# An H3-plus-MLP kernel on one core: the hand-written order of its second part is written anew

## The chip, the cores and the metric

The kernel runs on one core of a Trainium2 chip. The time is device microseconds for one execution; before the change three runs gave a median of 238.91 us (238.69 to 239.14). Five engines work side by side: TensorE (PE, with its weight loads shown apart as PEld), VectorE (DVE), ScalarE (ACT), GpSimd (POOL), and SyncE (SP), which here only issues DMA transfers.

## The reference: what is computed

Four residual blocks follow each other on x of shape 1 x 2048 x 512. Two kinds alternate, A, B, A, B, with the same weights each time.

```
A: k_shift = 4-tap causal FIR of k along the sequence, a filter per channel
   kv      = k_shift * v
   y       = causal convolution of kv with ssm_k (2048 taps per channel, by FFT) + kv * ssm_D
   x       = x + layernorm(x) * y
B: h = gelu_tanh(layernorm(layernorm(x)) @ w1 + b1)      # 512 -> 1376
   x = x + h @ w2 + b2                                    # 1376 -> 512
```

k, v and ssm_k do not depend on x, so y is the same in both A blocks and is computed once. Everything is bfloat16 with f32 accumulation.

## The kernel before, in words

The sequence is cut in two halves of 1024 positions. For each half the long convolution is done as a transform by matmuls: a first stage (`stage1`, matmuls at L557), a second stage (`stage2`, matmuls at L569), a product in the frequency domain on DVE (`tt`, L468), and two inverse stages (`inverse1`, L674, and `inverse2`, L696), which give y. The FIR is a set of matmuls with diagonal weights (`shift_pair`, L642, in the second half), and its product with v is DVE's L651. For the second half the products of the transforms ("p2" and "x2_1" in the code) are added by DVE ("sum", L468 too), and `inverse1` reads the sums. Each first- or second-stage result leaves PSUM through `evac`, which is ACT's L473 or DVE's L474.

The MLP works on row tiles of 128 positions, put together into row blocks: in the first half two blocks of one tile and seven of two tiles, in the second half four blocks of four tiles. For each block: statistics (`stats`: DVE L810 and L811, then POOL L815 and L817 for 1/sqrt, then L820, whose form on DVE the profile shows as L822 and whose form on POOL as L825), the normalisation (`norm`: ACT L835 or DVE L836), the product with y and the residual sum (DVE L468), statistics and normalisation again, a transpose (a DMA transpose issued by SP at L879, for the first two tiles PE's L887), then 11 groups of four matmuls of the first MLP matmul (L899), each followed by ACT's gelu (L904), and 11 matmuls per row tile of the second (L933, in three groups of 4, 4 and 3), followed by DVE's residual sum (L937). The last row tile is cut into pieces of 256, 128 and 128 columns (L922, L926).

Nothing is scheduled at run time. Every operation is recorded once in a `Prog`, and three tables decide the rest. `SEQ` lists all 1185 operations in one global order; each engine executes its own in that order. `ENGS` has a letter for each operation that two engines can do. `BANKS` gives each PSUM tile its place in the eight banks; a tile that gets a bank waits until the previous owner was read. `sync` then derives every semaphore wait from the data and from the banks. So a table changes when things happen and on which engine, and never what is computed.

```
self.seq = [self.ops[i] for i in self.SEQ]
o.eng = ... {"a": ACT, "v": DVE, "p": POOL}[next(choice)]      # letters of ENGS
t.base = int(b)                                                # digits of BANKS
```

Of the kernel before, what the change touches and what calls it, by code (L numbers as in the profile page):

```python
# [36 lines left out]
class Prog:  # L37
# [62 lines left out]
    ENGS = (  # L100
            "avapapvpaavvaavaavaaaaavvvvapvppvavvavaavaavvaaaaaaaavaaaaaaaaavaavaaaaaapvpvaaaaaaaaaaaaaaaaaaaaaaaaaaa"
            "aappappaavpvppaappvvppaapvaappaappaappaappaappavppvappaapvaappvvppvappvapvvvaapvavavvvvavvvvvvvvpvvvvvvv"
            "aavvpvaavvvvavvv")
    BANKS = (
            "45704306202464200000627236026646246464226006402420624644066042640262264660244620204426464644246204266020"
            "22247020226337626301520172570440464475725755436672367720371021321620440063513741720454430362521124671007"
            "27743140661373223714364027332203342000120556367705202105351567170234501404453107474")

    def __init__(self, nc):
        self.nc = nc  # L110
# [863 lines left out]
```

## Time and profile before

| | |
|---|---|
| median of 3 runs | 238.91 us (238.69 to 239.14) |
| the profiled execution's own time | 238.14 us |
| its span in the trace | 236.3 us |
| busy: PE, PEld, DVE, ACT, POOL | 222.5, 146.9, 179.2, 159.2, 49.1 us |
| matmuls recorded | 2743 |
| granted TensorE clock | 1.00 of full speed over the whole span |

The span is what the trace shows between the first and the last instruction; 1.84 us of the profiled execution's time lie outside it. Start times below are microseconds from the span's start. The chain of waits (called "the chain" below) follows the last instruction back, at each step to what released it. A few matmul records are missing from the trace, and each missing one looks like a gap of some 50 ns in PE's busy time though PE went on.

### The profile page before, as it was taken

The numbers are of one execution on the slowest core, as the hardware profiler recorded it, in microseconds if no ns is written. First come the engines' busy times: TensorE is split into PE (matmuls) and PEld (weight loads), VectorE is DVE, ScalarE is ACT, GpSimd is POOL, SyncE is SP. The second block draws the span as 40 slices with busy tenths as digits, with TensorE's granted clock in tenths as the row PEclk, the third lists the DMA queues.
The fourth block names the chain that finished last, engine by engine and source line by source line (L and its number), as shares of the span: only waits on it lengthen the run. The fifth ranks groups of instructions, "written<-read, shape, count | busy, mean of one in ns | idle before, by whom it ended". The sixth has DMA issues, their size and how long they took to land.

```text
span 236.3 us, 6496 instructions
## 1 busy us (share of the span) xinstructions
PE 222.5 (94%) x2743; PEld 146.9 (62%) x2765; DVE 179.2 (76%) x364; ACT 159.2 (67%) x254; POOL 49.1 (21%) x104
## 2 busy tenths in 40 slices
PE   6898787998999999999999999999999999999995
PEld 3787677876958578567867567644444444444444
DVE  0679979999999999999999899593179779521122
ACT  2963899998969679999787999556047204913520
POOL 1450020914222215321204432101020120100000
PEclk9999999999999999999999999999999999999999
DMA  6999879893869620032500212401200030173102
GB/s 213 299 390 385 304 213 287 250 284 69 171 124 254 142 47 3 0 49 52 172 0 6 44 26 53 105 0 29 60 1 3 13 76 0 22 114 133 44 0 92
DMA packets 41113, 26.77 MB, mean 113 GB/s; under 512 B 23702, under 2 KB 33788, under 8 KB 41084
## 3 DMA queue, kind: packets, MB, share of 16 engines
q1 hardware_dynamic: 40786, 26.20, 40.0%
q8 instruction: 22, 0.36, 0.6%
q10 hardware_dynamic: 298, 0.16, 0.3%
q14 instruction: 7, 0.06, 0.1%
HBM read 15.07 MB, written 2.10 MB: 73 GB/s over the span
## 4 chain that ended last, share of the span: by engine, by line
PE 65%; DVE 17%; ACT 7%; SPq 4%; DMA 3%; issue 2%; DVEq 0%
PE ps L933 27%; PE ps L899 27%; DVE ar L468 12%; ACT ar L473 6%; DMA ar<-in_A_v_dram 3%; SPq L453 3%; PE ps L569 2%; PE ps L557 2%; PE ps L696 2%; PE ps L674 2%; DVE ar L474 1%; ACT ar L904 1%; DVE ar L620 1%; PE ps L922 1%; DVE sm L810 1%
## 5 line engine op out<-in xcount | busy, mean ns | idle before, releaser
L904 ACT ACTIVATE ar<-ps,sm 128x256 bf16<-128x256 f32 (+5 forms) x143 | 65.8, 523 | 37.5 <-PE ps L899 37.3
L899 PE MATMUL ps<-ar 128*128 128x256 bf16 (+5 forms) x568 | 81.8, 297 | 0.5 <-ACT ar L473 0.2
L473 ACT ACTIVATE ar<-ps 128x1024 bf16<-128x1024 f32 (+3 forms) x77 | 71.8, 1003 | 14.0 <-PE ps L557 4.7
L933 PE MATMUL ps<-ar 128*128 128x512 bf16 (+1 forms) x325 | 76.2, 379 | 1.4 <-issue 0.6
L899 PEld LDWEIGHTS ps<-ar 128*128 128x128 bf16 (+1 forms) x572 | 52.7, 100 | 27.8 <-ACT ar L904 0.7
L468 DVE TENSOR_TENSOR ar<-ar 128x512 bf16<-128x512 bf16 (+3 forms) x105 | 62.9, 636 | 3.0 <-ACT ar L835 1.7
L933 PEld LDWEIGHTS ps<-ar 128*128 128x128 bf16 (+1 forms) x341 | 32.5, 98 | 35.9 <-ACT ar L904 0.4
L810 DVE BATCH_NORM_STATS2 sm<-ar 128x6 f32<-128x512 bf16 x64 | 42.4, 682 | 0.4
L937 DVE TENSOR_TENSOR ar<-ar,ps 128x512 bf16<-128x512 bf16 x31 | 20.6, 678 | 29.2 <-PE ps L933 29.0
L835 ACT ACTIVATE ar<-ar,sm 128x512 bf16<-128x512 bf16 x33 | 25.9, 808 | 13.2 <-DVE sm L822 10.6
L817 POOL TENSOR_TENSOR sm<-sm 128x2 f32<-128x2 f32 (+2 forms) x26 | 21.4, 822 | 32.5 <-DVE sm L815 30.7
L815 POOL TENSOR_SCALAR sm<-sm 128x2 f32<-128x2 f32 (+2 forms) x21 | 6.1, 293 | 91.2 <-DVE sm L811 90.9
L557 PE MATMUL ps<-ar 128*64 128x128 bf16 x512 | 17.5, 221 | 2.4 <-POOL ar L468 1.1
L569 PE MATMUL ps<-ar 128*128 128x64 bf16 x512 | 17.9, 193 | 1.7 <-ACT ar L473 1.3
L569 PEld LDWEIGHTS ps<-ar 128*128 128x128 bf16 x512 | 16.6, 98 | 3.8 <-ACT ar L473 1.8
L474 DVE CAST ar<-ps 128x1024 bf16<-128x1024 f32 x13 | 15.8, 1219 | 2.9 <-PE ps L569 1.8
L557 PEld LDWEIGHTS ps<-ar 128*64 128x64 bf16 x512 | 14.8, 110 | 5.0 <-POOL ar L468 1.2
L674 PE MATMUL ps<-ar 64*128 64x64 bf16 (+1 forms) x384 | 12.6, 203 | 0.5 <-ACT ar L473 0.3
L674 PEld LDWEIGHTS ps<-ar 64*128 64x128 bf16 (+1 forms) x384 | 11.9, 114 | 1.9 <-ACT ar L473 1.2
L836 DVE TENSOR_SCALAR ar<-ar,sm 128x512 bf16<-128x512 bf16 x31 | 12.0, 407 | 0.8 <-POOL sm L825 0.5
L767 DVE SCALAR_TENSOR_TENSOR ar<-ar,sm,ps 128x512 bf16<-128x512 bf16 x16 | 10.7, 743 | 0.4 <-PE ps L569 0.4
L811 DVE BATCH_NORM_AGGREGATE sm<-sm 128x2 f32<-128x6 f32 x64 | 10.1, 171 | 0.6
(42 smaller groups left out, 90.0 us busy)
## 6 DMA issues: line engine op xcount, KB each, us to landing
ar<-tab_s SPq DMA_DIRECT2D x16, 256.0 KB, 7.9
ar<-ar SPq DMA_DIRECT2D x16, 256.0 KB, 4.3
ar<-in_A_ssm_k_dram SPq DMA_DIRECT2D x8, 256.0 KB, 6.7
ar<-in_A_q_dram SPq DMA_DIRECT2D x8, 256.0 KB, 4.6
ar<-in_A_v_dram SPq DMA_DIRECT2D x8, 256.0 KB, 6.3
out_dram<-ar SPq DMA_DIRECT2D x7, 256.0 KB, 2.4
ar<-in_B_w_dram SPq DMA_DIRECT2D x4, 344.0 KB, 5.2
ar<-in_B_w_dram SPq DMA_DIRECT2D x5, 256.0 KB, 4.4
```

The costliest lines, as they stand in the source:

```text
L468: return P.op(eng, lambda e: e.tensor_tensor(o, a, b, op), dur, reads=[a, b] + list(more), writes=[o])
L473: return e.activation(dst, src(), AF.Copy)
L557: r = e.matmul(Q(tl, 64 * ri, 64, i * 128, [1, 128]), w, m, start=True, stop=True)
L569: r = e.matmul(Q(tl, 0, 128, i // 8 * 512 + i % 8 * 4, [32, 16], [1, 4]), w, m, start=True, stop=True)
L674: r = e.matmul(Q(tl, 0, 128, i, *([32, 16], [1, 4]) if split else ([1, 128],)), w, m, start=n == 0, stop=n == 1)
L810: P.op(DVE, lambda e, sj=sj, x=x: e.bn_stats(sj, x), 600.0, reads=[x], writes=[sj])
L817: P.op(POOL, lambda e: e.tensor_tensor(r, v, hf, ALU.pow), 420.0 + 149.0 * n, reads=[v, hf], writes=[r])
L835: return e.activation(o, x, AF.Identity, bias=u, scale=r)
L899: r = e.matmul(Q(tl, 0, rows, 0, [1, w]), a, m, start=dk == 0, stop=dk == 3)
L904: P.op(ACT, lambda e, dst=dst, tl=tl, rows=rows, bias=bias, w=w: e.activation(dst, Q(tl, 0, rows, 0, [1, w]), AF.Gelu_apprx_tanh, bias=bia ...
L933: r = e.matmul(Q(tl, 0, 128, 0, [1, 512]), ins[fc][0], ins[fc][1], start=fc == 0, stop=fc == 10)
L937: P.op(DVE, lambda e, x=x, tl=tl: e.tensor_tensor(x, x, Q(tl, 0, 128, 0, [1, 512]), ALU.add), 604.0, reads=[x], writes=[x], tile=tl)
```

## The change

Only the three tables differ. The first 330 entries of `SEQ` are the same, which is everything up to about 60.7 us of the trace; the other 855 are in a new order, on every engine. 23 operations behind that point go to another engine: of the ACT-or-DVE normalisations nine go from DVE to ACT and four from ACT to DVE; of the small statistics steps that DVE or POOL can do, seven go from DVE to POOL and three the other way. The banks of most tiles behind the same point are new. No operation is added or removed, and the shapes are the same. A line or two of each table:

```diff
     SEQ = (
         ...
-        424, 413, 404, 421, 259, 450, 405, 422, 288, 451, 408, 480, 423, 452, 415, 456, 483, 460, 457, 481, 446, 453,
...
+        424, 387, 413, 422, 425, 259, 408, 421, 452, 288, 466, 409, 480, 418, 453, 416, 467, 483, 448, 417, 481, 456,
...
     ENGS = (
...
-            "aappappaavpvppaappvvppaapvaappaappaappaappaappavppvappaapvaappvvppvappvapvvvaapvavavvvvavvvvvvvvpvvvvvvv"
-            "aavvpvaavvvvavvv")
+            "aappappaavpvppaappvvppaapvaappaappaapvaappaappavppvappaappaappvvppaappvappaaavvvvvaappvaaapvvvavpvvvavpp"
+            "aavvvvvaavvvvvvv")
     BANKS = (
-            "45704306202464200000627236026646246464226006402420624644066042640262264660244620204426464644246204266020"
...
+            "45704306202464200000627236026646246464226006402420624644066042640262264600644466440666002624266260062444"
...
```

**PE, where the first transform stage of the second half (L557, `stage1` with tag "x1_1") stands among the MLP's matmuls (L899 and L933).** Before, from the second group of L557 to the last:

```order
L557 MATMUL ps<-ar 64x128 x16
L899 MATMUL ps<-ar 128x256 x36
L899 MATMUL ps<-ar 96x256 x4
L899 MATMUL ps<-ar 128x256 x4
L899 MATMUL ps<-ar 96x256 x4
L899 MATMUL ps<-ar 128x256 x4
L557 MATMUL ps<-ar 64x128 x32
L933 MATMUL ps<-ar 128x512 x4
L899 MATMUL ps<-ar 128x256 x4
L557 MATMUL ps<-ar 64x128 x32
L933 MATMUL ps<-ar 128x512 x8
L557 MATMUL ps<-ar 64x128 x32
```

And now, from the second group of L557 to the last:

```order
L557 MATMUL ps<-ar 64x128 x48
L933 MATMUL ps<-ar 128x512 x8
L557 MATMUL ps<-ar 64x128 x48
L933 MATMUL ps<-ar 128x512 x7
L557 MATMUL ps<-ar 64x128 x16
```

In both orders one more group of 16 stands ahead of these, right behind L642. So the eight steps of 16 matmuls are in five groups before and in four now, and the L899 matmuls that stood between them stand ahead of them.

**DVE, the frequency-domain products and sums of the second half (L468 with 128x32x64) that the inverse transform (L674) waits for.** Before:

```order
L468 TENSOR_TENSOR ar<-ar 128x32x64 x2
L811 BN_AGGR sm<-sm 128x2
L468 TENSOR_TENSOR ar<-ar 128x32x64 x3
L822 SCALAR_TENSOR_TENSOR sm<-sm 128x2
L468 TENSOR_TENSOR ar<-ar 128x32x64
L937 TENSOR_TENSOR ar<-ar,ps 128x512
L468 TENSOR_TENSOR ar<-ar 128x32x64 x6
```

And now:

```order
L811 BN_AGGR sm<-sm 128x2
L468 TENSOR_TENSOR ar<-ar 128x32x64 x3
L937 TENSOR_TENSOR ar<-ar,ps 128x512
L468 TENSOR_TENSOR ar<-ar 128x32x64 x2
L937 TENSOR_TENSOR ar<-ar,ps 128x512
L468 TENSOR_TENSOR ar<-ar 128x32x64 x10
```

The small statistics steps (L811, L822) have left the middle of the run, and the last ten products and sums stand in one piece where six stood.

**POOL, the statistics of the row block whose L811 is the one just shown (the eighth block, "q7" in the code).** Before:

```order
L825 TENSOR_SCALAR sm<-sm 128x1 x2
L815 TENSOR_SCALAR sm<-sm 128x2
L817 TENSOR_TENSOR sm<-sm 128x2
L851 MEMSET ar 1x512
L815 TENSOR_SCALAR sm<-sm 128x2
L817 TENSOR_TENSOR sm<-sm 128x2
```

And now:

```order
L815 TENSOR_SCALAR sm<-sm 128x2
L817 TENSOR_TENSOR sm<-sm 128x2
L825 TENSOR_SCALAR sm<-sm 128x1 x2
L815 TENSOR_SCALAR sm<-sm 128x2
L851 MEMSET ar 1x512
L817 TENSOR_TENSOR sm<-sm 128x2
```

The step that was L822 on DVE is now the L825 pair on POOL: the block has four POOL instructions in a row where it had two.

More of the change, by code (lines that the diff above doesn't have):

```diff
@@ L58 @@
         244, 257, 584, 403, 585, 443, 249, 410, 412, 586, 406, 207, 411, 250, 444, 213, 407, 420, 293, 445, 258, 414,
[41 rows of a table removed]
[41 rows of a table added]
     ENGS = (
             "avapapvpaavvaavaavaaaaavvvvapvppvavvavaavaavvaaaaaaaavaaaaaaaaavaavaaaaaapvpvaaaaaaaaaaaaaaaaaaaaaaaaaaa"
-            "aappappaavpvppaappvvppaapvaappaappaappaappaappavppvappaapvaappvvppvappvapvvvaapvavavvvvavvvvvvvvpvvvvvvv"
-            "aavvpvaavvvvavvv")
+            "aappappaavpvppaappvvppaapvaappaappaapvaappaappavppvappaappaappvvppaappvappaaavvvvvaappvaaapvvvavpvvvavpp"
+            "aavvvvvaavvvvvvv")
     BANKS = (
-            "45704306202464200000627236026646246464226006402420624644066042640262264660244620204426464644246204266020"
-            "22247020226337626301520172570440464475725755436672367720371021321620440063513741720454430362521124671007"
-            "27743140661373223714364027332203342000120556367705202105351567170234501404453107474")
+            "45704306202464200000627236026646246464226006402420624644066042640262264600644466440666002624266260062444"
+            "46206466216237643301320727321504123101100322332716373063445423545175402012133355426403067156573421254373"
+            "47061653171314250227620662421047670120016563423216502311505064403200454166210125364")
     def __init__(self, nc):
```

80 rows, old and new, of the table SEQ are left out of this document.

## The prediction, made before the changed kernel was run

> **What bounds the kernel now.** I read the page first, then the busy time by stretches, then the chain of waits, and last the weight loads' waits. The page says who works all the time:
>
> ```profile
> span 236.3 us, 6496 instructions
> PE 222.5 (94%) x2743; PEld 146.9 (62%) x2765; DVE 179.2 (76%) x364; ACT 159.2 (67%) x254; POOL 49.1 (21%) x104
> PEclk9999999999999999999999999999999999999999
> ```
>
> PE is busy for 94% at full clock. The change begins at about 60.7 us, so I cut the time behind it into stretches that end where the kernel's character changes (123.26 us is the end of DVE's run of products and sums, 160 us the point from which only MLP work is left). The columns are the stretch, its length, and each engine's busy time:
>
> ```profile
> 60.00:80.00 20.00, 19.79 (x334) 14.72 (x339) 19.59 (x44) 16.28 (x41) 4.18 (x12) 1.00 0.83 190
> 80.00:100.00 20.00, 19.52 (x305) 14.68 (x297) 19.91 (x35) 17.89 (x32) 6.64 (x14) 1.00 0.13 22
> 100.00:123.26 23.26, 23.10 (x264) 17.07 (x265) 22.99 (x30) 21.11 (x39) 4.25 (x7) 1.00 0.30 69
> 123.26:160.00 36.74, 36.15 (x442) 23.04 (x446) 32.65 (x90) 28.55 (x48) 8.93 (x18) 1.00 0.17 38
> 160.00:230.00 70.00, 69.68 (x320) 31.98 (x325) 34.53 (x89) 28.16 (x45) 5.94 (x8) 1.00 0.18 42
> 230.00:236.30 6.30, 3.77 (x39) 2.79 (x38) 2.01 (x5) 0.00 (x0) 0.00 (x0) 1.00 0.27 86
> ```
>
> PE's idle time is 0.21, 0.48, 0.16, 0.59 and 0.32 us in the first five stretches. In the fifth no other engine is busy for half of the time and the chain is PE throughout, so I take its 0.32 us for missing records: they are not to be had. That leaves 1.44 us. An order can neither remove a matmul nor shorten one, so **1.44 us and what the switches between kinds of matmul cost is all that this change can gain**, some 0.6% of the time. What it can lose has no such bound: DVE is busy 62.49 of the 63.26 us from 60 to 123.26 us, and PE has little to do without it at the seam between the halves.
>
> **The change part by part.** *Switches.* A piece of the chain of waits (start, length, work), where L557 stands alone between L899:
>
> ```profile
> 83.81 2.62 PE ps L899 x24
> 86.43 0.57 PE ps L557 x16
> 87.00 5.78 PE ps L899 x52
> 92.79 1.01 PE ps L557 x32
> ```
>
> Twenty-four L899 take 2.62 us, 0.109 each; 52 of them should take 5.68 and take 5.78, so coming back costs 0.10. A lone group of 16 L557 takes 0.57 us, two together 1.01: the second one costs 0.44, so going in costs 0.13. A round trip is 0.2 us, and five groups become four: **-0.2 us**. The number of groups of L642 and of L674 does not change. At worst the rest of the cost stays hidden behind other waits: 0 to -0.2.
>
> *The front, 60.7 to 70 us.* Here PE does the first half's small groups of L899 faster than ACT does the gelus that empty their banks. The waits of the weight loads in this stretch, and the chain:
>
> ```profile
> PEld ps L899 <- ACT ar L904: 0.5, 2, 0.3
> ...
> 60.53 1.74 ACT ar L904 x6
> ...
> 62.27 0.63 ACT ar L904 x2
> 62.91 0.05 issue
> 62.95 0.84 PE ps L899 x12
> ```
>
> The chain lies on ACT's gelus until 62.91 us, so PE is paced by them. A weight load waits in 0.5 us of which PE, which has earlier matmuls in its pipe, loses a part. The new order has the first L569 after 36 more L899 instead of 48, and eight L899 instead of four before the next one, so ACT gets its pause earlier. Nothing in it removes a gelu. Bounds: all 0.5 comes back, or the waits move and grow by half of that (+0.25). I take **-0.15 us**, nearer to the lower half of the gain since ACT remains full.
>
> *The seam, L674.* Each of the eight steps fills two PSUM banks and waits for ACT to empty earlier ones. PE's timeline there, and the waits of its weight loads from 100 to 160 us:
>
> ```profile
> 124.47 2.56 PE L674 MATMUL ps<-ar 64*128 64x64 bf16 x128
> 127.19 1.46 PE L933 MATMUL ps<-ar 128*128 128x512 bf16 x6 [0.16 <-DVE sm L811]
> 128.58 2.56 PE L674 MATMUL ps<-ar 64*128 64x64 bf16 x128
> 131.30 1.89 PE L933 MATMUL ps<-ar 128*128 128x512 bf16 x8 [0.16 <-issue]
> ...
> PEld ps L674 <- ACT ar L473: 0.8, 3, 0.4
> ```
>
> Both groups take 2.56 us, with up to 0.8 us of waits for ACT in them, and the gaps of 0.16 us behind them. The new order keeps two groups of four steps with seven L933 between them, and all eight evacuations on ACT. The same loop of PE, ACT and bank stands there again: I take **-0.05 us**, between -0.4 (half of the waits go) and +0.4 (half as many again).
>
> *Ahead of the seam, DVE against PE.* Between the divergence and the first L674 the two orders hold the same PE work, and the same DVE work but for one L822 that leaves and one that comes. What is in cover there:
>
> ```profile
> 116.37 7.23 DVE L468 TENSOR_TENSOR ar<-ar 128x2048 bf16<-128x2048 bf16 x7
> 123.52 0.69 DVE L810 BATCH_NORM_STATS2 sm<-ar 128x6 f32<-128x512 bf16 x1
> ```
>
> DVE's last sum ends before 123.52 and L674 starts at 124.47: 0.95 us of cover. PE comes up to 0.4 us earlier by the terms above, which leaves about 0.5. So this costs **nothing** as long as DVE is not more than 0.5 us later than now; if it is, L674 waits for it, and behind L674 the inverse, the next statistics and the next row block's transposes.
>
> *Normalisations and statistics moved between engines* shift DVE's load in the second half to ACT and POOL. There PE has 69.68 of 70 us of work queued and DVE and ACT half of theirs: **nothing**, covered by the m2 matmuls (L933); without that cover a four-tile step on POOL instead of DVE would be 1 us on the path of its block. On SP's queue the transposes keep their order but for neighbours, and three stores of finished rows move behind the last transposes:
>
> ```profile
> out_dram<-ar SPq DMA_DIRECT2D x7, 256.0 KB, 2.4
> ```
>
> Nothing waits for them but the end, some 20 us later: nothing. *The end*, behind 230 us, has the same pieces (three of L922, the sums, the last stores): 0.
>
> The sum: -0.2 - 0.15 - 0.05 = **-0.4 us**. From the profiled execution's own 238.14 us (236.3 of span, 1.84 around it) this makes 237.7; the median of the runs lies 0.77 above that execution, so **238.5 us** is what I expect of the median, 0.17% under 238.91. About 0.2%, 0.48 us, is what a measurement of this kernel can tell from no change, so my forecast lies inside it, near its edge.
>
> **The rivals.** *The gain is given back.* The new order puts L569 steps singly between L899 from 101 to 116 us, each with an evacuation on ACT, which is busy 21.11 of 23.26 us there: a gelu that stands behind an evacuation frees its bank later by that much. Ten places at 0.03 to 0.06 us are +0.3 to +0.6, and the time is 238.7 to 239.2, around 238.9. For it speaks ACT's load, against it that PE's idle time in that stretch is only 0.16 us today, with the same evacuations on ACT.
>
> *DVE is late at the seam (slower).* The products wait for evacuations (their row in DVE's timeline, the first pair of the second half's products):
>
> ```profile
> 102.90 2.36 DVE L468 TENSOR_TENSOR ar<-ar 128x2048 bf16<-128x2048 bf16 x2 [0.23 <-ACT ar L473]
> ```
>
> In the new order the second-stage steps come to PE one by one, and the product of each can start only when its evacuation is through. If DVE waits in this run as for this pair but at six places instead of one, that is 6 x 0.23 = 1.4 us later, 0.9 beyond the cover; L674 waits, and with it the block behind it. It decides from 0.5 us of delay; at 1.4 the time is 238.5 + 0.9 = 239.4, with the front's gain gone too 239.6. Against it: the new order leaves DVE nothing else between the products, so that none is queued behind a statistic.
>
> *GpSimd is shut out (slower).* The profile shows what a run of two-input products on DVE can do to a small POOL instruction:
>
> ```profile
> 40.24 6.11 DVE ar L468 x10
> ...
> 41.32 5.41 POOL L632 COPY ar<-ar 128x3 bf16<-128x3 bf16 x2 [7.74 <-PE ps L557]
> ...
> 98.44 0.33 POOL L815 TENSOR_SCALAR sm<-sm 128x2 f32<-128x2 f32 x1 [3.68 <-DVE sm L811]
> ...
> 111.23 1.07 POOL L815 TENSOR_SCALAR sm<-sm 128x2 f32<-128x2 f32 x1 [8.82 <-DVE sm L811]
> 112.39 1.57 POOL L817 TENSOR_TENSOR sm<-sm 128x2 f32<-128x2 f32 x1
> ```
>
> Two copies of three elements take 5.41 us and are through only when the ten L468 are; the same L815 takes 0.33 us alone and 1.07 beside the products. The new order has the four POOL instructions of one block start at this run, and ten L468 in one piece at its end (10 x 1.2 = 12 us). If the last of the four is shut out until the run ends at about 123.3 us, the two normalisations on ACT that need it hold up ACT from about 119, and with it the gelus whose banks PE wants: some 4 us, 242.5. It decides if the four are not through when the ten begin, near 112 us. Between the block's L811 and the ten stand five products and two L937, some 7 us, so the four would each have to lose more than the 1.07 and 1.57 us of the rows at 111 us. The Trainium skill ("SBUF — State Buffer", section "Who interferes with whom") says that a VectorE tensor_tensor with both inputs in SBUF contends with a GpSimd instruction that reads SBUF, and that whoever issues first holds the shared ports for the whole instruction. By that rule each of the four waits for one product, 1.2 us, and all are done before the ten begin: no cost. The rows at 111 us agree with it, and the row at 41.32, which outlasts eight products, is worse than it.
>
> *All of it comes back.* If the new order removed every wait, 1.44 us: 237.5. Against it the loop at L674, which stands as it was.
>
> **How the numbers follow.** My forecast (238.2 to 238.7) gets 0.40, the gain given back 0.24, a larger gain (237.5 to 238.2) 0.12, DVE late at the seam 0.18, GpSimd shut out 0.06. Faster by over 0.2% means below 238.43: the larger gain and 0.26 of the forecast, 0.38. Within 0.2%: the other 0.14 and the gain given back, 0.38. Slower: 0.24. The range is 237.7 to 239.6: it leaves out the hold, the far end of the larger gain and half of the late DVE, about 0.17 in all. The likeliest case's own range is 238.2 to 238.7.
>
> **What would show it.** The switches: four groups of L557 in PE's timeline, and a lone group still at 0.57. The front: the weight loads' wait for L904 between 60 and 70 us under 0.5 us. The seam: L674 still 2.56 us a group, its first start about 0.3 us earlier than 124.47, and DVE's last sum before it. GpSimd: the L815 to L825 of that block through before 112 us. In the stretch from 160 to 230 us PE 69.7 us busy as now. The prediction is wrong if PE's idle time behind 60 us has grown by more than half a microsecond, or fallen by more than one.

## The result, and the profile after

| | before | after |
|---|---|---|
| median on the same chip | 238.91 us (238.06 to 240.06, 9 runs) | 237.40 us (236.53 to 238.17, 9 runs) |
| ratio | 1 | 0.9929 (0.9904 to 0.9955) |
| the profiled execution's own time | 238.14 us | 237.62 us |
| its span | 236.3 us | 235.8 us |

The kernel became faster by 0.71%, some 1.5 us. The prediction had 238.5 us and a range from 237.7: the direction of its sum was right, the gain is larger, and the time lies 0.3 us below the range. In 33 of 325 executions of these kernels the granted clock is 0.993 instead of 1.0 and the time is longer, by 1.4 us on the mean, so a median of some ten runs moves by a few tenths with their number.

The page of the kernel after, who works all the time:

```profile
span 235.8 us, 6520 instructions
PE 223.4 (95%) x2765; PEld 146.6 (62%) x2765; DVE 177.0 (75%) x355; ACT 161.7 (69%) x259; POOL 55.2 (23%) x117
```

All 2765 matmuls are recorded in this trace; before, 22 records were missing. Records go missing with the trace and not with the kernel: two of the four repeats of the kernel after (below) lack 22 as well. The busy time by stretches (stretch, length, then the busy time of PE, PEld, DVE, ACT and POOL):

```profile
60.00:80.00 20.00, 20.00 (x330) 14.90 (x331) 19.97 (x44) 16.42 (x42) 4.36 (x13) 1.00 0.85 178
80.00:100.00 20.00, 20.00 (x313) 14.89 (x301) 19.68 (x36) 17.90 (x33) 7.57 (x11) 1.00 0.24 38
100.00:123.26 23.26, 23.26 (x278) 17.18 (x278) 22.61 (x28) 21.63 (x38) 5.66 (x11) 1.00 0.27 70
123.26:160.00 36.74, 36.63 (x447) 23.01 (x446) 30.62 (x83) 31.14 (x52) 12.06 (x27) 1.00 0.15 30
160.00:229.50 69.50, 69.50 (x327) 32.09 (x326) 34.00 (x84) 27.76 (x46) 6.61 (x12) 1.00 0.19 46
```

PE's idle time in these stretches fell from 1.76 to 0.11 us. That is not 1.65 us of gain, nor any part of it. A repeat of the kernel after (a_rep1) that lacks 22 records is idle for 1.75 us in the same five stretches (busy for 167.75 of 169.50 us), although its steps start at the same times, to 0.01 us, as in the trace that shows 0.11. So nearly all of the 1.76 us before is missing records too, some 0.08 us for each, and not the 50 ns given ahead. What the order gained is read from the starts of PE's steps. At some places both orders have done exactly the same set of PE steps, and there the two can be compared. Microseconds from the same L899 at 60 us, worked out from the starts of PE's matmuls (at 131 us of a weight load, where the matmul's record is missing) in three traces of the kernel before and two of the kernel after:

```
                            before   repeat   repeat    after   repeat   difference
77.8 us, behind the FIR     17.914   17.911   17.912   17.684   17.683     -0.23
83.4 us                     23.575   23.571   23.572   23.298   23.297     -0.28
121.1 us, ahead of L674     61.277   61.280   61.271   60.651   60.650     -0.63
127.6 us                    67.765   67.768   67.756   67.143   67.142     -0.62
131.1 us, behind the seam   71.216   71.218   71.214   70.603   70.598     -0.62
191.5 us                   131.606  131.608  131.605  130.990  130.989     -0.62
the last matmul's end      173.967  173.969  173.963  173.351  173.350     -0.62
```

The stretch behind 60 us is the same from execution to execution to 0.01 us, and the change is worth 0.62 us in it. At 103.9 us, behind the last L557 group, the two profiled executions are 0.50 us apart (43.990 against 43.486, at the first step behind the same work). So 0.28 us come up to 83 us, 0.23 from there to 104 us, 0.12 from there to 121 us, and nothing at the L674 groups or behind them: the first L674 starts 0.62 us earlier already (64.612 against 63.989). From the last matmul to the span's end it is 2.52, 2.74 and 2.52 us before, and 2.40 and 2.41 us after (2.39 to 2.41 in five traces).

The front first. The weight loads of the kernel after wait for nothing at all between 60 and 70 us; the 0.5 us of waits for L904 are gone. ACT's timeline there, before and then after, shows how:

```profile
60.53 4.15 ACT L904 ACTIVATE ar<-ps,sm 128x128 bf16<-128x128 f32 x15
64.53 0.84 ACT L835 ACTIVATE ar<-ar,sm 128x512 bf16<-128x512 bf16 x1
```

```profile
60.73 3.59 ACT L904 ACTIVATE ar<-ps,sm 128x128 bf16<-128x128 f32 x13
64.17 0.85 ACT L835 ACTIVATE ar<-ar,sm 128x512 bf16<-128x512 bf16 x1
```

ACT's run of gelus is two shorter, and PE, which has eight L899 between its L569 instead of four, no longer waits for a bank. Between 104 and 121 us a wait of the same kind got shorter, that of an L569 for a gelu. The weight loads' waits from 100 to 160 us, before and then after:

```profile
PEld ps L569 <- ACT ar L904: 0.4, 1, 0.4
```

```profile
PEld ps L569 <- ACT ar L904: 0.2, 1, 0.2
```

Before, that L569 starts at 107.67 us, 0.73 us behind the first of the three L933 ahead of it, where three L933 ahead of the next L569 (at 109.92) take 0.65: it costs PE 0.08 of the 0.12 us. The L557 groups in the chain of the kernel after (start, length, work):

```profile
93.78 1.46 PE ps L557 x48
95.24 1.83 PE ps L933 x8
97.07 1.46 PE ps L557 x48
98.53 1.62 PE ps L933 x7
100.16 0.57 PE ps L557 x16
```

Three together cost 1.46, a lone one 0.57 as before. And the seam, PE's timeline and then DVE's:

```profile
124.05 2.56 PE L674 MATMUL ps<-ar 64*128 64x64 bf16 x128
126.55 1.69 PE L933 MATMUL ps<-ar 128*128 128x512 bf16 x7
128.17 2.57 PE L674 MATMUL ps<-ar 64*128 64x64 bf16 x128
```

```profile
115.51 8.15 DVE L468 TENSOR_TENSOR ar<-ar 128x2048 bf16<-128x2048 bf16 x7
123.58 0.68 DVE L937 TENSOR_TENSOR ar<-ar,ps 128x512 bf16<-128x512 bf16 x1
```

DVE's last sum ends at 123.66 us and the first L674 starts at 124.05: 0.39 us of cover are left. Counted in the same way it was 0.87 before (116.37 + 7.23 is 123.60, and L674 started at 124.47); the 0.95 of the prediction counts from the start of DVE's next instruction, and so counted 0.47 is left. The groups themselves take what they took.

### The profile page after: what moved, and what is told of

It reads as the page before. It is cut to its first block, busy times and chain, and to the rows that moved or that the text cites. A ratio compares the mean times of both kernels' runs of the same rounds, so it can differ in the third digit from the quotient of the medians.

```text
span 235.8 us, 6520 instructions
## 1 busy us (share of the span) xinstructions
PE 223.4 (95%) x2765; PEld 146.6 (62%) x2765; DVE 177.0 (75%) x355; ACT 161.7 (69%) x259; POOL 55.2 (23%) x117
## 4 chain that ended last, share of the span: by engine, by line
PE 77%; DVE 7%; ACT 6%; SPq 4%; DMA 4%; issue 1%; DVEq 0%
PE ps L899 33%; PE ps L933 32%; ACT ar L473 6%; PE ps L569 4%; DMA ar<-in_A_v_dram 4%; DVE ar L468 4%; SPq L453 3%; PE ps L674 2%; PE ps L696 2%; DVE ar L620 2%; PE ps L557 2%; DVE ar L474 2%; PE ps L922 1%; PE ps L642 1%; SPq L463 0%
## 5 line engine op out<-in xcount | busy, mean ns | idle before, releaser
L904 ACT ACTIVATE ar<-ps,sm 128x256 bf16<-128x256 f32 (+4 forms) x143 | 64.8, 525 | 35.1 <-PE ps L899 34.8
L473 ACT ACTIVATE ar<-ps 128x1024 bf16<-128x1024 f32 (+3 forms) x77 | 71.6, 1003 | 14.7 <-PE ps L557 6.2
L899 PE MATMUL ps<-ar 128*128 128x256 bf16 (+4 forms) x572 | 81.0, 297 | 0.2 <-ACT ar L473 0.2
L933 PE MATMUL ps<-ar 128*128 128x512 bf16 (+1 forms) x341 | 78.3, 379 | 0.0
L899 PEld LDWEIGHTS ps<-ar 128*128 128x128 bf16 (+1 forms) x572 | 52.7, 100 | 26.1 <-ACT ar L473 0.3
L468 DVE TENSOR_TENSOR ar<-ar 128x512 bf16<-128x512 bf16 (+3 forms) x105 | 62.6, 641 | 4.5 <-ACT ar L473 3.0
L933 PEld LDWEIGHTS ps<-ar 128*128 128x128 bf16 (+1 forms) x341 | 32.5, 98 | 36.5 <-ACT ar L904 0.4
L810 DVE BATCH_NORM_STATS2 sm<-ar 128x6 f32<-128x512 bf16 x64 | 42.6, 682 | 0.4
L835 ACT ACTIVATE ar<-ar,sm 128x512 bf16<-128x512 bf16 x38 | 30.2, 823 | 12.6 <-DVE sm L822 10.5
L815 POOL TENSOR_SCALAR sm<-sm 128x2 f32<-128x2 f32 (+2 forms) x22 | 7.6, 347 | 109.0 <-DVE sm L811 108.4
L937 DVE TENSOR_TENSOR ar<-ar,ps 128x512 bf16<-128x512 bf16 x31 | 20.4, 679 | 16.1 <-PE ps L933 16.1
L557 PE MATMUL ps<-ar 128*64 128x128 bf16 x512 | 17.2, 221 | 2.8 <-POOL ar L468 1.2
L569 PE MATMUL ps<-ar 128*128 128x64 bf16 x512 | 18.3, 193 | 1.3 <-ACT ar L473 0.9
L569 PEld LDWEIGHTS ps<-ar 128*128 128x128 bf16 x512 | 16.9, 98 | 3.2 <-ACT ar L473 1.4
L557 PEld LDWEIGHTS ps<-ar 128*64 128x64 bf16 x512 | 14.8, 110 | 5.6 <-ACT ar L473 1.6
L836 DVE TENSOR_SCALAR ar<-ar,sm 128x512 bf16<-128x512 bf16 x26 | 9.9, 406 | 5.1 <-POOL sm L825 5.0
L825 POOL TENSOR_SCALAR sm<-sm 128x1 f32<-128x1 f32 x40 | 13.2, 347 | 1.9
L674 PE MATMUL ps<-ar 64*128 64x64 bf16 (+1 forms) x384 | 12.6, 203 | 0.5 <-ACT ar L473 0.3
L674 PEld LDWEIGHTS ps<-ar 64*128 64x128 bf16 (+1 forms) x384 | 11.9, 114 | 1.9 <-ACT ar L473 1.2
```

Source lines behind the costliest of these rows:

```text
L468: return P.op(eng, lambda e: e.tensor_tensor(o, a, b, op), dur, reads=[a, b] + list(more), writes=[o])
L473: return e.activation(dst, src(), AF.Copy)
L557: r = e.matmul(Q(tl, 64 * ri, 64, i * 128, [1, 128]), w, m, start=True, stop=True)
L569: r = e.matmul(Q(tl, 0, 128, i // 8 * 512 + i % 8 * 4, [32, 16], [1, 4]), w, m, start=True, stop=True)
L674: r = e.matmul(Q(tl, 0, 128, i, *([32, 16], [1, 4]) if split else ([1, 128],)), w, m, start=n == 0, stop=n == 1)
L810: P.op(DVE, lambda e, sj=sj, x=x: e.bn_stats(sj, x), 600.0, reads=[x], writes=[sj])
```

## The experiments

**The two kernels again, word for word, twice each on one chip.** Two theories on why the medians lie further apart than the two profiled executions (0.52 us): T1, that PE waits behind 60 us in some executions, and T2, that the part ahead of it varies.

> The kernel before, unchanged, to see how its executions differ. Two theories. T1 (waits behind the change): in a typical execution the kernel before waits more behind 60.7 us than in the one I read; then the first L899 behind that point starts at 60.6 to 60.9 us in every trace, and the stretch from there to the last matmul, 173.1 us in the trace I read, is 173.5 to 174.5 here. T2 (luck of the early part): executions differ in the common part; then that start moves by up to 0.8 us from trace to trace and the stretch behind it stays at 173.1 +- 0.2. Both expect a ratio of 1.000 +- 0.003 against itself.

> As b_rep1, a second trace of the kernel before. T1: stretch behind the change 173.5 to 174.5 us, start 60.6 to 60.9. T2: stretch 173.1 +- 0.2, start differing by up to 0.8 us from 60.7.

> The changed kernel, unchanged, a second trace. Its first trace had the start at 60.81 and 172.60 us behind it. T1: the stretch is 172.4 to 172.8 again, since the new order does not wait, and the gain over the kernel before in the same call is 1.2 to 1.8 us. T2: the stretch is 172.6 +- 0.2, the start moves, and the gain over more runs comes down to 0.5 to 0.9 us.

> As a_rep1, a third trace of the changed kernel: T1 172.4 to 172.8 us behind a start at 60.6 to 60.9; T2 the same stretch behind a start that moves.

Measured: before 238.70 and 238.75 us, ratios to the shared runs of the kernel before 0.9986 (0.9962 to 1.0011) and 0.9991 (0.9966 to 1.0016); after 237.85 and 237.68 us, ratios 0.9950 (0.9929 to 0.9972) and 0.9936 (0.9907 to 0.9965). The traces gave the table above (the expectations count from a later L899, so that their 173.1 and 172.6 us are its 173.97 and 173.35), and with it the answer for the profiled executions: nothing varies behind 60 us. The profiled times of the kernel before, 237.99 and 239.34 us, differ by 1.35 us; the step at 60 us starts at 59.39 in the one and at 60.97 us in the other, 1.58 apart, and what follows is the same to 0.01 us, but for 0.23 less behind the last matmul. What varies lies ahead of 60 us, and the landing of the first loads is only a part of it: the last load of v lands at 18.14 and at 18.63 us, 0.49 of the 1.58. But 0.62 + 0.2 us do not make the 1.2 to 1.5 us between the medians. Two theories on the rest follow: D, that it arises ahead of 60 us, and X, that executions which were not profiled wait behind 60 us.

**The two orders mixed at the seam.** Of the 1185 entries, 713 of one kernel (708 in the other mixture) and the rest of the other; each step keeps the engine and the bank that it has where it comes from, with the banks behind the join renamed so that no two owners overlap.

```diff
-    SEQ = (all 1185 entries in the old order)
+    SEQ = (the first 713 of the new order, then what is left in the old order)        # h_first
+    SEQ = (the first 708 of the old order, then what is left in the new order)        # h_second
```

> The new order up to just ahead of the first L674, the old order behind it (the sets of operations done by then differ by one). Theory D (what the order does is the same in every execution, and the six traces show all of it: -0.62 us from PE at 60 us to its last matmul, -0.21 from the last matmul to the span's end; the rest of the medians' difference, some 0.5 us, arises ahead of 60 us, where all kernels are the same, in the arrival of the first loads): from PE at 60 us to the last matmul this kernel is 0.5 to 0.6 us shorter than the kernel before, from the last matmul to the end 2.5 to 2.75 us as before. Theory X (in executions that were not the profiled ones the old order waits somewhere behind 60 us): if the place is ahead of the seam, the median is down by all of 1.1 to 1.3 us, though the trace shows 0.6.

> The old order up to just ahead of the first L674, the new order behind it. Theory D: from PE at 60 us to the last matmul at most 0.1 us shorter than the kernel before, the end behind the last matmul 2.4 us instead of 2.5 to 2.75, and the median 0.2 to 0.3 us under the kernel before, give or take what the first loads do. Theory X with its place behind the seam: a median that is down by 0.8 us or more.

Measured: h_first 238.93 us, ratio 1.0005 (0.9980 to 1.0030), and h_second 239.65 us, ratio 1.0026 (0.9995 to 1.0058). In the trace of h_first PE is 0.63 us ahead at 121 us, as the kernel after is, and at 127.6 us all of it is gone. The weight loads' waits from 112 to 135 us say where:

```profile
PEld ps L674 <- DVE ar L937: 0.8, 1, 0.8
PEld ps L674 <- ACT ar L473: 0.6, 2, 0.4
PEld ps L674 <- DVE ar L468: 0.4, 1, 0.4
```

The first line is the join's own doing: one L674 got the bank of an m2 tile whose L937 stands late in the old order of DVE, PE waits 0.68 us there, and neither parent's trace has such a wait. The third line costs nothing: it stands word for word in the kernel after. So neither mixture met either theory, and what they tell is another thing: a gain ahead of the seam is worth nothing where the bank that comes next is not free earlier, too. h_second lost 0.58 us at its join: its second L674 group stands behind three L933 instead of seven, and its weight load waits 1.00 us for ACT's L473, PE 0.51. Behind the joins both run in step with the kernel whose order they follow.

**A later start for PE, so that the loads have landed.**

```diff
-        for i in range(7):
+        for i in range(27):
             r = e.matmul(Q(tl, 0, 128, 0, [1, 512]), z[:, :128], z, start=True, stop=True)
```

> The kernel before with 27 instead of 7 matmuls at L511 (the matmuls on zeros at the start, some 0.4 us each), so that PE begins some 8 us later and the first loads have arrived by then. Theory D: most of the spread goes (a standard deviation of 0.7 us becomes 0.3 or less), and the kernel after with the same change lies 0.8 us under this one. Theory X: the spread stays as it is, and the two lie 1.3 us apart.

> The kernel after with 27 instead of 7 matmuls at L511. Theory D: 0.8 us under the kernel before with the same change, both with a standard deviation of 0.3 us or less. Theory X: 1.3 us under it, with the spread as without the change.

Measured: 241.80 us with a standard deviation of 0.31 us (6 runs) for the kernel before, 241.59 us with 0.95 us (6 runs) for the kernel after: the first as D has it, the second not, and the distance is neither's. The trace of a_warm shows what happened to the new order. PE's timeline, and the wait of the weight loads from 150 to 160 us:

```profile
154.53 1.03 PE L696 MATMUL ps<-ar 128*128 128x512 bf16 x4
155.82 2.55 PE L899 MATMUL ps<-ar 128*128 128x512 bf16 x11 [0.27 <-DMA ar<-ar]
```

```profile
PEld ps L899 <- DMA ar<-ar: 0.8, 1, 0.8
```

The first L899 of the second half's first block waits for its last transpose (L879), which landed 4.13 us after its issue instead of the 2.49 us of the kernel after, and PE is 0.44 us later from there to the end. So a wait behind 60 us, of the kind that X supposes, does exist, but here in the new order: in b_warm the last two transposes of the same block take 4.43 and 3.56 us, and the stretch is 173.97 us as without. It depends on which transpose is late and on what PE has ahead of the block.

**Only the common part; a little more time ahead of the transposes; other banks.** The first ends the program behind the last PE step that both orders share, and leaves out the rest of the output and three transfers that nothing in it reads.

```diff
-        self.seq = [self.ops[i] for i in self.SEQ]
+        self.seq = [self.ops[i] for i in self.SEQ[:330] if i not in (207, 291, 293)] + [self.ops[-1]]   # cut
```
```diff
                     for o in self.order[e]:
+                        if e == SP and o.tag[:1] == "z" and o.tag not in seen:                          # b_late, a_late
+                            seen.add(o.tag)
+                            for _ in range(12):
+                                eng.wait_ge(sems[PE], 1)
```

> Only the part that is the same in all kernels: the first 330 entries of the order (three transfers that nothing in it reads are left out), and a store of 32 KB behind PE's last matmul of it, so the output is not the reference's. It measures how much of the spread arises ahead of 60 us. Theory D (all of it arises there): a standard deviation of 0.7 us, as that of the kernel before. Theory X (part of it arises behind 60 us: a DMA transpose of L879 that is in flight while a block of 16 KB of instructions is fetched lands 0.7 to 2 us later, and the kernel before has places where its first L899 comes only 0.1 to 0.6 us behind the landing, at 87 and 106 us, the kernel after none of these): 0.5 us or less, at most that of the kernel after (0.5).

> The kernel before with 12 waits on a semaphore that is long reached ahead of the first L879 of each block on SP's queue, which should make each block's transposes some 0.5 us later. Theory X: PE waits for them ahead of the first L899 at 106 us (cover 0.1 to 0.6 us), so that the stretch from 60 us to the last matmul grows by 0.2 to 0.5 us there, and the median by 0.3 to 0.8. Theory D (the landing of the transposes is of no account): no change beyond 0.1 in the stretch.

> The kernel after with the same 12 waits. Theory X: its cover at the same two blocks is 0.8 to 2.1 us, so nothing at 87 and 106 us, and the distance to the kernel before with the same change grows to 1.5 us or more. Theory D: both as without the waits, 1.3 us apart.

> The kernel before with the banks 0 to 7 renamed to 6, 7, 4, 5, 2, 3, 0, 1 throughout: the same order, the same waits, another program. If the 0.5 us that the traces do not show belong to the order (theory X), the mean stays at that of the kernel before, within 0.3 us, and the spread too. If each program has a start of its own by chance, mean and spread may lie anywhere between those of the kernels before and after. In the trace, both: 173.97 us from PE at 60 us to the last matmul, as before.

Measured: cut 64.80 us (64.31 to 65.56, 6 runs), standard deviation 0.45 us; b_late 239.30 us, ratio 1.0015 (0.9990 to 1.0039); a_late 238.30 us, 0.9977 (0.9948 to 1.0005); b_banks 239.08 us, 1.0017 (0.9986 to 1.0047). The common part alone varies by 1.25 us in six executions, but one of them, 65.56 us, makes most of that: without it the standard deviation is 0.26. So six are too few to tell theory D's 0.7 from theory X's 0.5. The twelve waits of a block became six instructions of some 0.06 us each, and where SP's timeline shows them (at 133 us) five of the six were through before the transposes' data was ready. The transposes are 0.07 us later, not 0.5, so that b_late and a_late delayed nothing that matters (173.97 and 173.38 us in the stretch, as their parents): they do not test X. They do serve as other programs with the same order, and so does b_banks (173.97): the two with the old order have the median of the kernel before, to 0.3 us, and the mean of a_late lies 0.65 us (standard error 0.3) under that of the kernel before, where the traces say 0.8 and the medians 1.2 or more. That speaks against an unseen gain of the order, but no louder than its error allows.

**Once more on another chip, and three mixtures with cleaner joins.** Here the joins were put where the banks behind them have the same owners in turn as in the kernel that they come from.

```diff
-    SEQ = (all 1185 entries in the old order)
+    SEQ = (the first 491 of the new order, then the old order)        # new_to_83
+    SEQ = (the first 750 of the new order, then the old order)        # new_to_131
+    SEQ = (the first 750 of the old order, then the new order)        # old_to_131
```

> The kernel after, once more, as a measure beside the three mixtures. Theory D (the whole of it is in the traces, 0.83 us): 0.6 to 1.0 us under the kernel before. Theory X (0.5 us more in executions that were not profiled): 1.2 to 1.5 us under it, as in the two comparisons so far. In the trace again 173.35 us from PE at 60 us to the last matmul.

> The new order up to 83 us of the trace (the front and the FIR behind it), the old one behind that. If the front's gain of 0.23 to 0.27 us outlives the old seam (its cover on DVE is 0.95 us), the stretch from PE at 60 us to the last matmul is 173.70 us instead of 173.97. If something at the seam that is not PE sets the end, it is 173.9 or more.

> The new order up to 131 us, that is with the front, the L557 groups and the seam, and the old order of the rest. Theory D: 173.35 us in the stretch, as the kernel after, 2.5 to 2.75 us behind the last matmul, as the kernel before, and the median 0.6 us under the kernel before. Theory X with its place ahead of 131 us: 1.1 us or more under it.

> The old order up to 131 us, the new order of the rest. Theory D: 173.97 us in the stretch, as the kernel before, 2.4 us behind the last matmul, as the kernel after, and the median 0.2 us under the kernel before. Theory X with its place behind 131 us: 0.7 us or more under it.

Measured: a_rep3 237.73 us, ratio 0.9980 (0.9956 to 1.0004); new_to_83 240.54 us, 1.0091 (1.0063 to 1.0118); new_to_131 239.22 us, 1.0029 (0.9998 to 1.0060); old_to_131 239.71 us, 1.0038 (1.0012 to 1.0064). All three mixtures are slower than both parents, and the expected stretches of 173.70, 173.35 and 173.97 us became 175.15, 174.26 and 175.05. Again it is the join. In new_to_131 PE is in step with the kernel after to 0.005 us until 130 us, and loses 0.91 us at one L674 (PE's timeline):

```profile
128.82 1.79 PE L674 MATMUL ps<-ar 64*128 64x64 bf16 x96
131.58 0.72 PE L674 MATMUL ps<-ar 64*128 64x64 bf16 x32 [0.97 <-ACT ar L473]
132.23 2.12 PE L933 MATMUL ps<-ar 128*128 128x512 bf16 x9
```

In new_to_83 two L899 wait 1.9 us for DVE's L937. So none of them tells what a part is worth alone. What they do show: from 132 us to its last matmul new_to_131, with the old order, stays 0.29 us behind the kernel before without a change of more than 0.002 us at the places where both have done the same, and old_to_131, with the new order, ends 1.08 us behind it as it was at 132 us. The two orders of the rest, with all the norms and statistics that were moved between engines, take the same time. The ends behind the last matmul are 2.71 and 2.80 us in the two mixtures with the old end and 2.40 us in the one with the new. But the old end does not always take longer: it is 2.40 us in b_banks and in b_warm, and 2.46 in b_late.

**One step moved in the kernel after, and a last repeat.**

```diff
-        643, 614, 625, 694, 649, 572, 623, 615, 277, 695, 621, 308, 314, 309, 281, 322, 315, 576, 647, 696, 573, 323,
+        643, 614, 625, 694, 649, 572, 623, 615, 277, 695, 621, 308, 314, 309, 281, 576, 322, 315, 647, 696, 573, 323,
```

> The kernel after with one PE step moved: a piece of L933 (entry 576) stands ahead of the last of three L557 of a group instead of behind it, so that four groups of L557 become five again. By the price of the prediction, 0.2 us for a round trip, the stretch from PE at 60 us to the last matmul is 173.54 us instead of 173.35, all of it at this place, and 0.1 us by half that price. If other waits hide it, 173.35. The median: 0.2 us above that of the kernel after on the same chip (not to be told apart).

> The kernel after a last time, beside a_split. Theory D: mean 0.83 us under that of the kernel before, give or take 0.3. Theory X: 1.3 us or more under it.

Measured: a_split 238.20 us, ratio 0.9983 (0.9951 to 1.0015), and a_rep4 237.12 us, 0.9932 (0.9906 to 0.9958). The chain of a_split at the place:

```profile
93.22 0.86 PE ps L933 x4
94.09 1.01 PE ps L557 x32
95.10 0.97 PE ps L933 x4
96.07 0.57 PE ps L557 x16
96.64 0.97 PE ps L933 x4
97.61 1.46 PE ps L557 x48
```

Up to the moved step the trace is in step with the kernel after to 0.003 us; behind it it is 0.22 us later, and stays so to the last matmul (173.57 against 173.34 to 173.35 us). The price of a round trip is 0.22 us: 0.57 + 1.01 for the two pieces against 1.46 for the one (0.12 for going in), and 0.97 for four L933 behind a group where four others take 0.86 (0.11 for coming back). The medians cannot tell 0.2 us.

**What stays open.** The comparisons of the unchanged kernel after with the kernel before gave, between the means, 1.68, 1.28, 1.53, 0.75 and 1.49 us (standard errors 0.17 to 0.29). All 52 executions against 159 of the kernel before: medians 237.64 and 238.80 us, 1.16 us apart (1.0 to 1.4). The traces account for 0.8. Other programs with the new order (a_late) or nearly (a_split) show no such excess beyond their errors. The profiled executions do not show it either: their step at 60 us starts between 59.39 and 60.97 us in three traces of the kernel before, and between 59.86 and 60.45 us in five of the kernel after. Whether the other 0.4 us are a start that suits this one program, or waits in executions that no profile shows, the runs do not settle.

## Why the prediction missed, step by step

- **Switches, -0.2: right.** Five groups became four. From 83 to 104 us, with all groups but the first in it, the order gained 0.23, and undoing one group cost 0.22.
- **The front, -0.15: right in mechanism, too small.** The waits for L904 went to zero, and PE gained 0.23 us by 77.8 us (0.28 by 83). The text left most of the 0.5 with a full ACT; that ACT is full mattered less than that its run of gelus was cut.
- **The seam, -0.05: nothing came.** The groups still take 2.56 and 2.57 us, and the waits for ACT are what they were. The first L674 comes 0.62 us earlier, counted from the step at 60 us, where 0.3 was expected, and the last matmul 0.62 too. What the prediction read as the seam's price was hardly one. The gaps of 0.16 us behind the groups are missing records: the trace of the kernel after that has them all shows no gap. And of the 0.8 us of waits, 0.43 stand ahead of a group. Ahead of either group, before and after, the weight load waits 0.42 or 0.43 us behind its L933, put down to L810, to L468 or to L473; that this is the change of kind itself is argued from the equal times.
- **The L569 steps from 104 to 121 us, put at nothing, and +0.3 to +0.6 in the rival: -0.12.** The rival's 0.03 to 0.06 us a place came from no row. PE loses less there than before, not more: it waits less for a gelu.
- **DVE's cover, 0.95 to about 0.5: right, 0.47 by the same count.** The rival of a late DVE did not come: only two L937 stand between the products, nearly as the prediction said against it. h_first shows what a bank held by a late L937 costs there.
- **GpSimd: through before 112 us, as forecast.** The four instructions beside the products, from POOL's timeline, with the same four in a quiet place ahead of them:

```profile
99.25 0.19 POOL L815 TENSOR_SCALAR sm<-sm 128x2 f32<-128x2 f32 x1 [3.70 <-DVE sm L811]
99.52 0.71 POOL L817 TENSOR_TENSOR sm<-sm 128x2 f32<-128x2 f32 x1
100.32 0.50 POOL L825 TENSOR_SCALAR sm<-sm 128x1 f32<-128x1 f32 x2
...
105.36 1.09 POOL L815 TENSOR_SCALAR sm<-sm 128x2 f32<-128x2 f32 x1 [2.47 <-DVE sm L811]
106.54 1.57 POOL L817 TENSOR_TENSOR sm<-sm 128x2 f32<-128x2 f32 x1
108.20 0.88 POOL L825 TENSOR_SCALAR sm<-sm 128x1 f32<-128x1 f32 x2
```

  They take from 105.36 to 109.08 us, 3.7 us instead of 1.6, with three products on DVE beside them (105.20 to 108.64 us), which is about half a product's 1.2 us of delay for each. That is within what the Trainium skill ("SBUF — State Buffer", section "Who interferes with whom") allows, a wait for one VectorE instruction at a time. The ten products start at 112.11 us, so what they would do to such an instruction was not met.
- **Moved norms and statistics, 0: right.** Nothing changes between 131 us and the last matmul, in the kernels or in the mixtures.
- **The end, 0: -0.2 on the mean.** "The same pieces" come in another order. The 256-column piece, in the middle before, is first now, so that its 64 KB store no longer runs beside the last 32 KB store. The DMA issues of the two kernels, before and then after (the last column is the time from issue to landing):

```profile
out_dram<-ar SPq DMA_DIRECT2D x1, 64.0 KB, 1.9
...
out_dram<-ar ACTq DMA_DIRECT2D x1, 32.0 KB, 1.6
```

```profile
out_dram<-ar SPq DMA_DIRECT2D x1, 64.0 KB, 2.8
...
out_dram<-ar ACTq DMA_DIRECT2D x1, 32.0 KB, 1.5
```

  The last store landed 1.6 us after its issue here and 1.9 us in a repeat of the kernel before, 1.5 us in the traces of the kernel after. In all, 0.2 us lie between the means of the three ends before and the five after. The neighbouring store is not enough of a cause: in b_banks and b_warm, which have the old order of the stores, the last store lands 1.50 us after its issue as well. The old end took 2.40 to 2.80 us in nine traces, the new one 2.39 to 2.41 in ten; why it varies stays open.
- **The step that failed: "the median of the runs lies 0.77 above that execution".** The sum should have been -0.8 instead of -0.4, and 238.14 - 0.8 + 0.77 would still have given 238.1, inside the range. But the profiled execution's distance to the other executions is no constant: over eighteen of the runs here it lay between 1.55 us below and 0.79 us above their mean. The kernel after's own lay 0.22 us above its median, so the step is off by 0.99 of the 1.1 us between 238.5 and 237.40, more than all terms of the sum together; the profiled executions themselves lie 0.52 us apart. The draw counts, too: over all its 52 executions the median of the kernel after is 237.64 us, only 0.06 below the range.
- **The bound, 1.44 us, and the sign set from it** ("wrong if PE's idle time has fallen by more than one"): it fell by 1.65 us in the profiled pair, by records that were missing and now are not, and by 0.01 us against a_rep1, which lacks as many. The 0.32 us were taken out for that reason, the others not, and the same reason held for them. So the bound bounded nothing: the 0.62 us came out of time that the rows call busy.

## What to carry to other kernels

Compare two orders at points where both have done the same work, counted from a common step: that gave 0.62 us to within 0.01 where whole executions vary by two. Compare starts of the same kind there, as a weight load starts ahead of its matmul, and count the matmul records before idle time of PE is believed. A single profiled execution is a draw, so its distance to the median is not to be carried over from one kernel to the next, and a difference below 1 us wants dozens of runs of both or the trace. Two good orders do not mix: each of five joins lost 0.5 us or more at once. Behind each stood a wait for a bank or for an evacuation that is shorter or missing in either order, so what an order gains at a place seems to be kept only if the banks and the engine queues behind it are in step with it.

## What the runs showed of the hardware

DMA transposes landed later when the core fetched instructions meanwhile. The DMA queues of the kernel before between 76 and 106 us and between 106.5 and 205 us, with the transposes' median time from issue to landing:

```profile
q8 instruction: 4, 0.07, 0.9%
...
ar<-ar SPq DMA_TRANSPOSE x6, 3.5
```

```profile
q8 instruction: 6, 0.10, 0.4%
...
ar<-ar SPq DMA_TRANSPOSE x19, 2.5
```

In nineteen traces, behind 85 us, 374 transposes had no instruction fetch in their first 2.5 us of flight, and none of them took more than 2.7 us. 85 had a fetch of 16 KB on q8 beside them; 69 of these took longer than 2.7 us, up to 4.5. No run moved a fetch alone. Loads and stores in flight made no such difference (58 of the 374 had one). The fetches stand at other places from kernel to kernel: one lies beside the transpose that was late in a_warm (issued at 151.65 us), and none beside it in the profiled execution of the kernel after. There the block's first weight load starts 1.0 us behind the landing, which covers only a part of such a delay.
